# Moving twelve gate mixes from the last attention steps into the value half, with three smaller changes of order

## The chip, the cores and the metric

The kernel runs on one core of one Trainium2 chip. The metric is device time in microseconds (us) of the whole launch, from the runs listed below. Engines are named TensorE (PE, with its weight loads PEld), VectorE (DVE), ScalarE (ACT), GpSimd (POOL) and SyncE (SP), which issues most DMAs in the order of its queue.

## What is computed

The reference is an attention whose scores are capped by a tanh, followed by a channel mix with a gate (batch 8, 12 heads, 448 positions, head size 64, model width 768, inner width 1024):

```
scores = cap * tanh(q k^T / sqrt(64) / cap)
attn   = softmax(scores);  x = attn v, heads side by side   # (8, 448, 768)
x_prev = x shifted by one position (zeros first)
xk = mu_k * x + (1 - mu_k) * x_prev;  xr = mu_r * x + (1 - mu_r) * x_prev
k  = relu(xk @ w_k);  v = k*k @ w_v;  r = sigmoid(xr @ w_r)
out = r * v
```

All is float32. Products that need it are made of three products of high and low parts (high x high, low x high, high x low).

## The kernel before

The order of all instructions is written out by hand; each engine runs its own in that order.

**Attention, steps 0 to 54.** 48 pairs of heads go through a software pipeline. The string `STEP` lists the operations of one step; an operation works on pair i, i-1 or i-2. Scores of pair i come in four groups (`S0` to `S3`), each followed on ScalarE by `tanh` and `exp` and on VectorE by `red` (row sums). In the next step `values` (`V`) makes the value product, `gather` collects the sums over SyncE (four small DMAs), `recip` inverts them on VectorE, and `rec_store` and `rec_load` (SyncE) spread the result over the partitions through device memory. In the step after that `norm` multiplies, `mix_old` (ScalarE) and `mix_new` (VectorE) make xk in the bank of the value product and so free it, `x_high` and `x_low` (GpSimd) split xk, and `gate_old` (GpSimd) and `gate_new` (VectorE) make xr, which `x_store` writes to device memory (`x_d`). Seven steps behind, `kpart` (`K`, four times in a step) makes the products with w_k; `relu` empties finished ones and `k_store` writes them (`k_d`). The weights are handed over as 64-bit numbers and are turned into float32 between these, until about step 40. There are no scores after step 47; steps 48 to 54 finish the pairs and the K products.

**The twelve early pairs.** For pairs 0 to 11 `gate_old` and `gate_new` are left out, and `x_store` writes the plain x to `raw_d`. Their gate mix is made later: from step 36 on `late_load` brings a tile back, `late_old` and `late_new` mix it in steps 37 to 48, and `late_store` writes it to `x_d`.

**Change of stage.** At step 49 (`tail`) the attention's buffers are closed, the halves of w_v are loaded (`w2_loads`, four DMAs of 768 KB), and `w2_prep` makes from them the seven factors of a Strassen product in high and low parts: 22 pieces, six behind each of the steps 50 to 53.

**Value half, then gate half.** 14 units of 256 tokens each. A unit has seven slots, one for each of seven products (`multiply`; 12 matmuls in the value half, 9 in the gate half). `ahead` prepares operands two slots early (high part on ScalarE, low part on VectorE), loads sources and, in the value half, squares them. `evacuate` empties the banks a slot after a product. w_r is loaded at the start of the value half (`w2_loads`, four DMAs of 576 KB) and prepared during it. A slot was emitted in this order: multiply, ahead, evacuate, stores.

Of the kernel before, what the change touches and what calls it, by code (L numbers as in the profile page):

```python
# [10 lines left out]
F32 = mybir.dt.float32  # L11
F32R = mybir.dt.float32r
AF = mybir.ActivationFunctionType
ALU = mybir.AluOpType
# [3 lines left out]
B, H, S, D = 8, 12, 448, 64  # L18
# [25 lines left out]
NB = 2 * S // 32  # L44
P1, P2, P3, P4, P5, P6, P7 = range(7)
LATE = 12
AT = NPAIR + 1 - LATE

STEP = """gather load_v weight_load more weight_low S0 S1 V S2 f f f f f tanh0 exp0 red0
weight_sum tanh1 exp1 red1 norm recip rec_store K qk_high qk_low tanh2 mix_old mix_new x_high x_low gate_old late_old relu k_store
K exp2 red2 weight_rest weight_sum relu k_store S3 K K tanh3 exp3 red3 gate_new late_new relu k_store weight_abs load_qk rec_load x_store late_store late_load weight_store"""


def f(ap):
    return ap.bitcast(F32)  # L60


class Body:
# [54 lines left out]
    def init_x(self, pool):  # L118
        self.X = []
        for j in range(2):  # L120
            x = pool.tile([P, S + 1], F32, name=f"x{j}", bufs=1)
            self.nc.vector.memset(x[:, 0:1], 0.0)
            self.X.append(x)
        self.xo = pool.tile([P, S + 1], F32, name="xo", bufs=1)
        self.nc.vector.memset(self.xo[:, 0:1], 0.0)

    def init_sums(self, pool):

# [185 lines left out]
            self.nc.sync.dma_start(self.raw_d[i], self.X[i % 2][:, 1:])  # L314

    def late_load(self, i):
        if i < LATE:
            self.nc.sync.dma_start(self.xo[:, 1:], self.raw_d[i])

    def late_old(self, i):  # L320
        if i < LATE:
            self.xl = self.up.tile([P, S], F32, name="xl", bufs=1)
            self.nc.gpsimd.tensor_scalar(self.xl, self.xo[:, 0:S], self.om["r"][:, i % NP:i % NP + 1], None, op0=ALU.mult)

    def late_new(self, i):
        if i < LATE:
            self.mix_gate(self.xo, self.xl, i % NP)

    def late_store(self, i):
        if i < LATE:  # L330
            self.nc.sync.dma_start(self.x_place(i), self.xl)

    def key_order(self):

# [116 lines left out]
        next(self.wgen)  # L451


    def w2_pool(self, kind, pool):
        n = (NF if kind == "v" else ND) // 2
        self.W2[kind] = lo, hi = {}, {}
        for x, w in (("l", lo), ("h", hi)):
            for m in (P1, P7, P3, P2, P5, P6, P4):
                w[m] = pool[x].tile([P, n, HN], F32R, name=f"w{kind}{x}{m}")

    def w2_loads(self, kind):
        lo = self.W2[kind][0]
        n, at = lo[P1].shape[1], (ND if kind == "v" else 0)
        for m, c, h in ((P1, 0, 0), (P7, 0, 1), (P3, n, 1), (P2, n, 0)):
            self.nc.sync.dma_start(f(lo[m]), self.w_d[at + c:at + c + n, :, h * HN:(h + 1) * HN].rearrange("c p n -> p c n"))

    def w2_split(self, kind, m, k, x=None):
        lo, hi = (w[m][:, k] for w in self.W2[kind])
        x = f(lo) if x is None else x
        self.nc.scalar.copy(hi, x)  # L470
        self.nc.vector.tensor_sub(lo, x, f(hi))

    def w2_prep(self, kind, scratch, k):

        a, b = scratch
        b11, b12, b22, b21 = (f(self.W2[kind][0][m][:, k]) for m in (P1, P7, P3, P2))
        for m, x, sub in ((P5, a, (a, b12, b11)), (P1, None, ()), (P6, b, (b, b22, a)), (P5, a, ()), (P4, a, (a, b21, b)),
                          (P6, b, ()), (P7, b, (b, b22, b12)), (P7, b, ()), (P2, None, ()), (P4, a, ()), (P3, None, ())):
            if sub:
                self.nc.vector.tensor_sub(*sub)  # L480
            else:
                self.w2_split(kind, m, k, x)
            yield
# [51 lines left out]
    def multiply(self, u, i):  # L535
        m, n = self.products(u)[i], self.half(u)
        hi, lo = self.ops.pop((u, i))
        wl, wh = (w[m] for w in self.W2["v" if u < NU else "r"])
        bank = {P1: 0, P2: 0, P6: 1, P7: 1, P5: 2, P3: 2, P4: 3}[m]
        first = (u, bank) not in self.ps  # L540
        if first:
            self.ps[u, bank] = self.ps_2.tile([P, 512], F32, name="ps2")
        o = self.ps[u, bank][:, 0:HN]
        last = not first or bank == 3
        todo = [(hi, w, c) for c in range(n) for w in (wh, wl)] + [(lo, wh, c) for c in range(n)]
        for k, (a, w, c) in enumerate(todo):
            self.nc.tensor.matmul(o, a[:, c, :], w[:, c, :], start=first and k == 0, stop=last and k == len(todo) - 1,  # L547
                                  skip_group_check=True)
# [65 lines left out]

    def slot(self, g):
        u, s = divmod(g, SLOTS)
        if u < 2 * NU:
            self.multiply(u, s)
            self.ahead(g)
        now, self.later = self.later, []  # L620
        if g and g <= 2 * NU * SLOTS:
            v, r = divmod(g - 1, SLOTS)
            self.evacuate(v, self.products(v)[r])
        for do, args in now:
            do(*args)


    def step(self, i, KS):

        nk = 0  # L630
        if self.maxima and i < NPAIR:
            self.row_maxima(i)
        pair = dict(load_qk=i + 3, qk_high=i + 2, qk_low=i + 2, load_v=i, S=i, tanh=i, exp=i, red=i)
        pair.update(dict.fromkeys("V gather recip rec_store rec_load".split(), i - 1))
        pair.update(dict.fromkeys("norm mix_old mix_new x_high x_low gate_old gate_new x_store".split(), i - 2))
        pair.update(dict.fromkeys("late_old late_new late_store".split(), i - AT), late_load=i + 1 - AT)
        for op in STEP.split():
            j = pair.get(op)
            op, g = (op[:-1], (int(op[-1]),)) if op[-1].isdigit() else (op, ())
            if op in pair:  # L640
                j = pair[op] if j is None else j
                if 0 <= j < NPAIR:
                    getattr(self, dict(S="scores", V="values").get(op, op))(j, *g)
            elif op == "K":
                if i >= LAG:
                    n = ((i - LAG) * 4 + nk) * KS
                    self.kpart(n, n + KS)
                nk += 1
            elif op == "f":
                if i <= NPAIR:  # L650
                    self.fill()
            elif op == "more":
                if i in (6, 7, 8, 9, 10):
                    self.weight_load()
            else:
                getattr(self, op)()

    def run(self):
# [7 lines left out]
        with ExitStack() as outer:  # L666
# [41 lines left out]
            tail = NPAIR + 1  # L708
            self.later = []
            first = -12  # L710
            for i in range(NPAIR + LAG):
                if i == tail:
                    self.weight_store()
                    assert self.w_next == NW and not (self.w_raw or self.w_abs or self.w_sum or self.w_low)
                    wst.close()
                    est.close()
                    ast.close()
                    tiles = dict(right, reuse_waits="tile")
                    self.w2_pool("v", {x: pool("w2v" + x, 1, **tiles) for x in "lh"})
                    self.srcp = pool("srcp", 2, **tiles)  # L720
                    self.sp = pool("sp", 1, **tiles)
                    self.evp = pool("evp", 1, **tiles)
                    self.w2_loads("v")
                    t = self.srcp.tile([P, NF, 2 * P], F32, name="src").rearrange("p (a n) t -> p a (n t)", a=2)
                    scratch = [t[:, j, :2 * HN].rearrange("p (n t) -> p n t", n=2) for j in range(2)]
                    prep = chain(*(self.w2_prep("v", scratch, slice(j, j + 2)) for j in (0, 2)))
                self.step(i, KS)
                if i == tail:
# [1 line left out]
                    sst.close()  # L730
                    self.opp = pool("opp", AHEAD + 1, **tiles)
                    self.ps_2 = pool("ps2", 6, space=PSUM, **right)
                else:
                    for _ in range(6 if i > tail else 0):
                        next(prep, None)
                if i > tail:
                    for g in range(first, min(first + 3, 0)):
# [8 lines left out]
            self.w2_pool("r", dict(l=w2r, h=w2r))  # L746
# [3 lines left out]
            st_pool = pool("st", 1, st)  # L750
            self.w2_loads("r")
            prep = self.w2_prep("r", [st_pool.tile([P, ND // 2, HN], F32, name=f"st{j}") for j in range(2)], slice(0, ND // 2))
            for g in range(2 * NU * SLOTS + 3):
                self.slot(g)
                if g > SLOTS and g % SLOTS == 3:
                    next(prep, None)
                if g == NU * SLOTS - 9:
                    assert next(prep, None) is None
# [58 lines left out]
```

## Time and profile before

| | |
|---|---|
| time, median of 3 runs | 981.52 us (979.04 to 981.6) |
| profiled execution, its own time | 978.96 us |
| its span, first to last instruction | 977.2 us |
| mean granted clock of TensorE | 0.977 |
| busy: TensorE, VectorE, ScalarE, GpSimd | 93%, 78%, 64%, 43% |

A page of the profile gives busy time as a share of the span; the end of a matmul is modelled, so a busy TensorE is not one at its peak. A row of a timeline has the start, the duration, the engine, the line, the operation with its tiles and, in brackets, how long the engine was idle before it and what ended that. A granted clock of 1.00 is 2.4 GHz and 0.50 is 1.2 GHz.

### The profile page before, as it was taken

What the parts mean: (1) busy time and instruction counts of PE and PEld (TensorE: products, weight loads), DVE (VectorE), ACT (ScalarE), POOL (GpSimd) and SP (SyncE); (2) the same over time, 40 slices, a digit from 0 to 9 for tenths busy, and PEclk for the clock granted to TensorE, in tenths of its full rate; (3) what the DMA queues carried; (4) which work ended last, traced back from release to release, by engine and by line L of the source; (5) the groups of instructions that cost most, each with busy time, mean ns of one, the idle gap of its engine ahead of it and who ended that gap; (6) DMA issues with size and microseconds to landing.
All of it is one profiled execution on the core that took longest, in us unless ns stands there. A gap on an engine that the chain in (4) does not pass through costs nothing. (4 is left out here: it accounts for less than half of the span.)

```text
span 977.2 us, 15124 instructions
## 1 busy us (share of the span) xinstructions
PE 907.9 (93%) x4986; PEld 719.7 (74%) x4986; DVE 757.6 (78%) x1262; ACT 624.0 (64%) x915; POOL 416.8 (43%) x362
## 2 busy tenths in 40 slices
PE   6778989999999999989889887999999999999996
PEld 3336656666666766656556676999999999999996
DVE  7999998888888888887776565777777766777775
ACT  7887668877887788777667244455546535554443
POOL 4666656666766776676664310000000013433330
PEclk9889999999999999999999999899999999999999
DMA  5556446665666666665553374433433436666663
GB/s 157 173 183 200 161 146 206 196 201 176 212 207 209 192 202 209 196 204 170 170 159 132 122 248 168 139 118 123 146 113 120 151 104 195 204 207 203 206 201 109
DMA packets 122008, 169.46 MB, mean 173 GB/s; under 512 B 22464, under 2 KB 106048, under 8 KB 121920
## 3 DMA queue, kind: packets, MB, share of 16 engines
q1 hardware_dynamic: 112704, 153.72, 49.7%
q10 hardware_dynamic: 9216, 14.68, 4.1%
q8 instruction: 41, 0.67, 0.3%
q14 instruction: 47, 0.39, 0.1%
HBM read 109.45 MB, written 56.14 MB: 169 GB/s over the span
## 5 line engine op out<-in xcount | busy, mean ns | idle before, releaser
L243 DVE TRANSPOSE_TENSOR_REDUCE r<-p 128x28 f32<-128x896 f32 (+1 forms) x240 | 216.0, 914 | 26.6 <-ACT p L217 22.6
L217 ACT ACTIVATE p<-p,cap_t 128x896 f32<-128x896 f32 x192 | 182.1, 948 | 13.4 <-ACT ko L361 8.6
L207 ACT ACTIVATE p<-s,scl_t 128x896 f32<-128x896 f32 x192 | 173.2, 902 | 21.2 <-PE s L199 13.8
L354 PE MATMUL kps<-xkh,wkh 128*128 128x448 f32 x384 | 147.6, 384 | 13.0 <-ACT ko L361 9.1
L354 PE MATMUL kps<-xkl,wkh 128*128 128x448 f32 x384 | 142.5, 371 | 1.1 <-POOL xkl L87 1.1
L354 PE MATMUL kps<-xkh,wkl 128*128 128x448 f32 x384 | 141.9, 370 | 0.0
L547 PE MATMUL ps<-wvh,hi 128*128 128x384 f32 x392 | 132.8, 339 | 7.0 <-ACT hi L531 5.6
L226 PE MATMUL pv<-p,rv 128*64 128x448 f32 x576 | 128.0, 582 | 5.1 <-DVE xk L283 4.6
L547 PE MATMUL ps<-wvl,hi 128*128 128x384 f32 x392 | 132.3, 337 | 0.0
L511 POOL TENSOR_TENSOR s<-src 128x384 f32<-128x384 f32 x14 | 14.3, 1025 | 275.3 <-DVE lo L532 271.3
L531 ACT CAST hi<-s 128x512 fp32r<-128x512 f32 (+1 forms) x112 | 63.5, 567 | 103.0 <-PE ps L547 87.9
L532 DVE TENSOR_TENSOR lo<-s,hi 128x512 fp32r<-128x512 f32 (+1 forms) x112 | 71.1, 635 | 63.4 <-ACT hi L531 53.5
L199 PE MATMUL s<-qkh 64*128 64x448 f32 (+1 forms) x336 | 84.8, 447 | 29.0 <-ACT p L207 24.2
L87 POOL TENSOR_TENSOR qkl<-rqk,qkh 128x960 fp32r<-128x960 f32 x47 | 107.7, 2291 | 3.9
L547 PE MATMUL ps<-wrh,hi 128*128 128x384 f32 x294 | 99.8, 340 | 5.6 <-DVE u L566 5.3
L428 POOL TENSOR_TENSOR wsq<-wa,wsq 128x384 f32<-128x384 f32 x44 | 44.7, 1016 | 136.0 <-DVE wsq L421 131.9
L199 PEld LDWEIGHTS s<-qkh 64*128 64x128 f32 (+1 forms) x336 | 36.8, 188 | 88.9 <-ACT p L207 41.0
L547 PE MATMUL ps<-wrl,hi 128*128 128x384 f32 x294 | 98.8, 336 | 0.0
L354 PEld LDWEIGHTS kps<-xkh,wkh 128*128 128x128 f32 x384 | 73.0, 190 | 34.8 <-issue 12.9
L531 ACT CAST hi<-src 128x512 fp32r<-128x512 f32 (+1 forms) x84 | 47.7, 568 | 69.5 <-PE ps L547 58.2
L226 PEld LDWEIGHTS pv<-p,rv 128*64 128x64 f32 x576 | 39.6, 144 | 71.0 <-issue 60.8
L278 ACT ACTIVATE pv<-x,om_k 128x448 f32<-128x448 f32 x48 | 30.6, 638 | 93.8 <-DVE x L268 93.8
(88 smaller groups left out, 1856.0 us busy)
## 6 DMA issues: line engine op xcount, KB each, us to landing
rqk<-qk SPq DMA_DIRECT2D x47, 480.0 KB
k_d<-ko ACTq DMA_DIRECT2D x64, 224.0 KB
src<-k_d SPq DMA_DIRECT2D x56, 256.0 KB
rv<-v SPq DMA_DIRECT2D x48, 256.0 KB
r<-rec_d SPq DMA_DIRECT2D x96, 112.0 KB
v_d<-o SPq DMA_DIRECT2D x56, 192.0 KB
src<-x_d SPq DMA_DIRECT2D x42, 256.0 KB
vl<-v_d SPq DMA_DIRECT2D x56, 192.0 KB
```

The source lines that it names most:

```text
L87: {"p": self.nc.gpsimd, "v": self.nc.vector}[e].tensor_sub(*a)
L199: nc.tensor.matmul(s[:, h, 0:S], qk[a][p, k], qk[b][p, 0:S], start=(n == 0), stop=(n == 2))
L207: self.nc.scalar.activation(p32, self.S.pop((i, g))[:, :n, 0:S], AF.Tanh, scale=self.scl_t)
L217: self.nc.scalar.activation(p32, p32, AF.Exp, scale=1.0 if self.maxima else self.cap_t)
L226: nc.tensor.matmul(pv[p, 0:S], v[:, g, h, :], ph[:, h, :], start=(g == 0), stop=False)
L243: self.nc.vector.tensor_reduce(out=out, in_=p32[p, h].rearrange("p h (b k) -> p (h b) k", k=32), axis=mybir.AxisListType.X, op=ALU.add, ap ...
L278: self.nc.scalar.mul(self.xold, self.X[i % 2][:, 0:S], self.om["k"][:, hp:hp + 1])
L354: nc.tensor.matmul(self.kps[fc][:, 0:S], w, m[:, dc, :], start=first, stop=last)
L428: {"p": self.nc.gpsimd, "v": self.nc.vector}[e].tensor_add(sq, f(a), sq)
L531: self.nc.scalar.copy(hi, x)
L532: self.nc.vector.tensor_sub(lo, x, f(hi))
L547: self.nc.tensor.matmul(o, a[:, c, :], w[:, c, :], start=first and k == 0, stop=last and k == len(todo) - 1, skip_group_check=True)
```

## The change

1. The late mixes leave the steps. `late_load` is emitted in slot 0 and the new `late_mix` in slot 2 of the value units 0 to 11. The multiply that GpSimd did is done by ScalarE. Their tiles come from a pool of that stage, and to make room for it the preparation of w_r works on one block of rows at a time, in 33 pieces instead of 11, emitted in three slots of a unit instead of one.
2. `relu` in the second line of `STEP` is emitted behind `tanh2` instead of behind the mixes.
3. The loads of w_v are emitted in step 48, behind `V` (`tail_open`), instead of at the start of step 49; six pieces of the preparation are emitted behind step 49 already.
4. In the gate half, `evacuate` is emitted ahead of `ahead` in slot 2.

```
-STEP = """gather load_v weight_load more weight_low S0 S1 V S2 f f f f f tanh0 exp0 red0
-weight_sum tanh1 exp1 red1 norm recip rec_store K qk_high qk_low tanh2 mix_old mix_new x_high x_low gate_old late_old relu k_store
-K exp2 red2 weight_rest weight_sum relu k_store S3 K K tanh3 exp3 red3 gate_new late_new relu k_store weight_abs load_qk rec_load x_store late_store late_load weight_store"""
+STEP = """gather load_v weight_load more weight_low S0 S1 V tail_open S2 f f f f f tanh0 exp0 red0
+weight_sum tanh1 exp1 red1 norm recip rec_store K qk_high qk_low tanh2 relu mix_old k_store mix_new x_high x_low gate_old
+K exp2 red2 weight_rest weight_sum relu k_store S3 K K tanh3 exp3 red3 gate_new relu k_store weight_abs load_qk rec_load x_store weight_store"""
...
-    def late_old(self, i):
...
-            self.nc.gpsimd.tensor_scalar(self.xl, self.xo[:, 0:S], self.om["r"][:, i % NP:i % NP + 1], None, op0=ALU.mult)
...
+    def late_mix(self, i):
+        x = self.latep.tile([P, S], F32, name="xl")
+        self.nc.scalar.mul(x, self.xo[:, 0:S], self.om["r"][:, i % NP:i % NP + 1])
+        self.mix_gate(self.xo, x, i % NP)
+        self.nc.sync.dma_start(self.x_place(i), x)
...
     def slot(self, g):
         u, s = divmod(g, SLOTS)
+        now, self.later = self.later, []
         if u < 2 * NU:
             self.multiply(u, s)
-            self.ahead(g)
-        now, self.later = self.later, []
+            if u < NU or s != 2:
+                self.ahead(g)
         if g and g <= 2 * NU * SLOTS:
             v, r = divmod(g - 1, SLOTS)
             self.evacuate(v, self.products(v)[r])
+        if NU <= u < 2 * NU and s == 2:
+            self.ahead(g)
+        if u < LATE and s == 0:
+            self.late_load(u)
+        if u < LATE and s == 2:
+            self.late_mix(u)
         for do, args in now:
             do(*args)
...
+    def tail_open(self, i):
+        if i == NPAIR:
+            self.weight_store()
...
+            self.open_tail()
...
+            def tail_open():
+                ast.close()
+                self.w2v = {"l": pool("w2vl", 1, **tiles)}
+                self.w2_pool("v", "l", self.w2v)
+                self.w2_loads("v")
+            self.open_tail = tail_open
...
-                else:
-                    for _ in range(6 if i > tail else 0):
+                if i >= tail:
+                    for _ in range(6):
                         next(prep, None)
...
-            prep = self.w2_prep("r", [st_pool.tile([P, ND // 2, HN], F32, name=f"st{j}") for j in range(2)], slice(0, ND // 2))
+            scratch = [st_pool.tile([P, 1, HN], F32, name=f"st{j}") for j in range(2)]
+            prep = chain(*(self.w2_prep("r", scratch, slice(j, j + 1)) for j in range(ND // 2)))
             for g in range(2 * NU * SLOTS + 3):
                 self.slot(g)
-                if g > SLOTS and g % SLOTS == 3:
+                if g > SLOTS and g % SLOTS in (1, 3, 5):
                     next(prep, None)
```

## Rows read from the trace of the kernel before

**Rows 1.** The page's first part: busy time, share of the span and instructions of each engine.

```profile
PE 907.9 (93%) x4986; PEld 719.7 (74%) x4986; DVE 757.6 (78%) x1262; ACT 624.0 (64%) x915; POOL 416.8 (43%) x362
```

**Rows 2.** Busy time by stretches: from and to, length, busy time of each engine with its instructions, granted clock, DMA share and rate. In order: steps 13 to 34; the K products of the last batch; the start of the value half; the rest of the value half; the gate half.

```profile
157.50:397.70 240.20, 239.37 (x1349) 162.95 (x1347) 204.66 (x352) 194.64 (x252) 160.53 (x132) 1.00 0.62 198
...
566.00:592.50 26.50, 25.90 (x120) 23.13 (x118) 19.25 (x22) 15.37 (x24) 2.10 (x2) 0.94 0.58 208
592.50:618.50 26.00, 18.60 (x85) 17.29 (x85) 13.43 (x22) 10.56 (x20) 0.00 (x0) 0.87 0.61 198
618.50:807.70 189.20, 189.20 (x1093) 189.10 (x1093) 137.51 (x216) 98.33 (x172) 4.32 (x4) 1.00 0.40 126
807.70:969.70 162.00, 156.28 (x884) 152.22 (x882) 120.82 (x222) 80.45 (x166) 56.18 (x52) 1.00 0.61 192
```

**Rows 3.** Timeline of VectorE: `mix_new` (line 283), which comes once in a step. The rows are those of pairs 11, 33, 34 and 45, in steps 13, 35, 36 and 47.

```profile
157.47 0.63 DVE L283 SCALAR_TENSOR_TENSOR xk<-x,mu_k,pv 128x448 f32<-128x448 f32 x1
...
397.73 0.63 DVE L283 SCALAR_TENSOR_TENSOR xk<-x,mu_k,pv 128x448 f32<-128x448 f32 x1
...
408.14 0.63 DVE L283 SCALAR_TENSOR_TENSOR xk<-x,mu_k,pv 128x448 f32<-128x448 f32 x1
...
544.98 0.63 DVE L283 SCALAR_TENSOR_TENSOR xk<-x,mu_k,pv 128x448 f32<-128x448 f32 x1
```

**Rows 4.** Timeline of SyncE's queue at the end of an earlier step (two rows) and of a late step (four rows), and three rows of the waits from 425 to 550 us (engine and line that waited, what it waited for, us in total, times, longest).

```profile
314.43 0.33 SPq L312 DMA_DIRECT2D x_d<-xg  x1
...
315.32 2.44 SPq L248 DMA_DIRECT2D sq<-r  x4
...
500.98 0.33 SPq L312 DMA_DIRECT2D x_d<-xg  x1
502.72 0.33 SPq L331 DMA_DIRECT2D x_d<-xl  x1
503.13 0.38 SPq L318 DMA_DIRECT2D xo<-raw_d  x1
503.57 2.44 SPq L248 DMA_DIRECT2D sq<-r  x4
...
ACT pv L278 <- DVE x L268: 28.7, 10, 4.3
DVE sr L252 <- DMA sq<-r: 19.6, 10, 2.7
...
PE kps L354 <- ACT ko L361: 5.3, 2, 3.0
```

**Rows 5.** Timelines around steps 47 to 49: SyncE's queue (the store of pair 45's gate mix, `gather`, `rec_store` and `rec_load` of pair 47, the loads of w_v), then VectorE (`recip` and `norm` of pair 47, the first piece of the preparation), then TensorE (the first K product that needs pair 47).

```profile
549.98 0.33 SPq L312 DMA_DIRECT2D x_d<-xg  x1
...
551.84 2.45 SPq L248 DMA_DIRECT2D sq<-r  x4
557.02 0.33 SPq L259 DMA_DIRECT2D rec_d<-rs  x1
558.64 1.12 SPq L264 DMA_DIRECT2D r<-rec_d  x2
...
563.38 2.30 SPq L465 DMA_DIRECT2D wvl<-w_d  x4
...
555.80 0.61 DVE L252 TENSOR_REDUCE sr<-sq 32x28 f32<-32x448 f32 x1 [4.30 <-DMA sq<-r]
...
562.84 0.62 DVE L268 TENSOR_TENSOR x<-pv,r 128x448 f32<-128x448 f32 x1
...
570.22 0.96 DVE L480 TENSOR_TENSOR src<-wvl,wvl 128x768 f32<-128x768 f32 x1 [1.40 <-DMA wvl<-w_d]
...
565.55 0.47 PE L354 MATMUL kps<-xkh,wkh 128*128 128x448 f32 x1 [3.77 <-POOL xkh L77]
```

**Rows 6.** Timelines at the start of the value half: ScalarE's queue (the last store of K products), SyncE's queue (loads of w_r, then the last quarter of unit 1's source), ScalarE (the square that reads it), TensorE (the last K product; the first matmul of unit 1).

```profile
598.72 0.33 ACTq L367 DMA_DIRECT2D k_d<-ko  x1
...
600.80 2.09 SPq L465 DMA_DIRECT2D wrl<-w_d  x4
602.93 0.49 SPq L491 DMA_DIRECT2D src<-k_d  x1
...
610.30 0.63 ACT L496 ACTIVATE src<-src 128x512 f32<-128x512 f32 x1 [7.58 <-DMA src<-k_d]
...
592.21 0.36 PE L354 MATMUL kps<-xkl,wkh 128*128 128x448 f32 x1
...
618.51 0.33 PE L547 MATMUL ps<-wvh,hi 128*128 128x384 f32 x1
```

**Rows 7.** The gate half: a low part on VectorE and TensorE's first matmul of slot 3 behind it, from the timelines, and one row of the waits from 807 to 977 us.

```profile
868.05 1.30 DVE L532 TENSOR_TENSOR lo<-src,hi 128x384 fp32r<-128x384 f32 x1 [0.50 <-ACT hi L531]
...
869.97 0.41 PE L547 MATMUL ps<-wrh,hi 128*128 128x384 f32 x1 [0.46 <-DVE u L566]
...
PE ps L547 <- DVE u L566: 5.3, 11, 0.7
```

**Rows 8.** Groups of instructions over the whole span: line, engine, operation, tiles, shapes and count, then busy us and mean ns of one, then the idle time before them and what ended it.

```profile
L566 DVE TENSOR_TENSOR u<-ps,p 128x384 f32<-128x384 f32 x56 | 30.7, 549 | 0.0
L278 ACT ACTIVATE pv<-x,om_k 128x448 f32<-128x448 f32 x48 | 30.6, 638 | 93.8 <-DVE x L268 93.8
...
L295 DVE SCALAR_TENSOR_TENSOR xl<-xo,mu_r,xl 128x448 f32<-128x448 f32 x12 | 12.5, 1045 | 3.6 <-POOL xl L323 3.6
```

More of the change, by code (lines that the diff above doesn't have):

```diff
@@ L46 @@
 LATE = 12
-AT = NPAIR + 1 - LATE
-STEP = """gather load_v weight_load more weight_low S0 S1 V S2 f f f f f tanh0 exp0 red0
-weight_sum tanh1 exp1 red1 norm recip rec_store K qk_high qk_low tanh2 mix_old mix_new x_high x_low gate_old late_old relu k_store
-K exp2 red2 weight_rest weight_sum relu k_store S3 K K tanh3 exp3 red3 gate_new late_new relu k_store weight_abs load_qk rec_load x_store late_store late_load weight_store"""
+STEP = """gather load_v weight_load more weight_low S0 S1 V tail_open S2 f f f f f tanh0 exp0 red0
+weight_sum tanh1 exp1 red1 norm recip rec_store K qk_high qk_low tanh2 relu mix_old k_store mix_new x_high x_low gate_old
+K exp2 red2 weight_rest weight_sum relu k_store S3 K K tanh3 exp3 red3 gate_new relu k_store weight_abs load_qk rec_load x_store weight_store"""
 def f(ap):
@@ L123, in init_x @@
             self.X.append(x)
-        self.xo = pool.tile([P, S + 1], F32, name="xo", bufs=1)
-        self.nc.vector.memset(self.xo[:, 0:1], 0.0)
     def init_sums(self, pool):
@@ L316, in late_load @@
     def late_load(self, i):
-        if i < LATE:
-            self.nc.sync.dma_start(self.xo[:, 1:], self.raw_d[i])
-    def late_old(self, i):
-        if i < LATE:
-            self.xl = self.up.tile([P, S], F32, name="xl", bufs=1)
-            self.nc.gpsimd.tensor_scalar(self.xl, self.xo[:, 0:S], self.om["r"][:, i % NP:i % NP + 1], None, op0=ALU.mult)
[L325 to L331, printed above, removed]
+        self.nc.sync.dma_start(self.xo[:, 1:], self.raw_d[i])
+    def late_mix(self, i):
[3 more added lines that the diff above has]
+        self.nc.sync.dma_start(self.x_place(i), x)
     def key_order(self):
@@ L451, in fill, with w2_pool @@
         next(self.wgen)
-    def w2_pool(self, kind, pool):
+    def w2_pool(self, kind, x, pool):
         n = (NF if kind == "v" else ND) // 2
[L456 to L459, printed above, removed]
+        self.W2[kind, x] = {m: pool[x].tile([P, n, HN], F32R, name=f"w{kind}{x}{m}") for m in (P1, P7, P3, P2, P5, P6, P4)}
     def w2_loads(self, kind):
-        lo = self.W2[kind][0]
+        lo = self.W2[kind, "l"]
         n, at = lo[P1].shape[1], (ND if kind == "v" else 0)
@@ L467, in w2_split @@
     def w2_split(self, kind, m, k, x=None):
-        lo, hi = (w[m][:, k] for w in self.W2[kind])
+        lo, hi = (self.W2[kind, a][m][:, k] for a in "lh")
         x = f(lo) if x is None else x
@@ L475, in w2_prep @@
         a, b = scratch
-        b11, b12, b22, b21 = (f(self.W2[kind][0][m][:, k]) for m in (P1, P7, P3, P2))
+        b11, b12, b22, b21 = (f(self.W2[kind, "l"][m][:, k]) for m in (P1, P7, P3, P2))
         for m, x, sub in ((P5, a, (a, b12, b11)), (P1, None, ()), (P6, b, (b, b22, a)), (P5, a, ()), (P4, a, (a, b21, b)),
@@ L537, in multiply @@
         hi, lo = self.ops.pop((u, i))
-        wl, wh = (w[m] for w in self.W2["v" if u < NU else "r"])
+        wl, wh = (self.W2["v" if u < NU else "r", a][m] for a in "lh")
         bank = {P1: 0, P2: 0, P6: 1, P7: 1, P5: 2, P3: 2, P4: 3}[m]
@@ L623, in slot @@
             self.evacuate(v, self.products(v)[r])
+        if NU <= u < 2 * NU and s == 2:
[4 more added lines that the diff above has]
+            self.late_mix(u)
         for do, args in now:
             do(*args)
+    def tail_open(self, i):
+        if i == NPAIR:
+            self.weight_store()
+            assert self.w_next == NW and not (self.w_raw or self.w_abs or self.w_sum or self.w_low)
+            self.open_tail()
     def step(self, i, KS):
@@ L635, in step @@
         pair.update(dict.fromkeys("norm mix_old mix_new x_high x_low gate_old gate_new x_store".split(), i - 2))
-        pair.update(dict.fromkeys("late_old late_new late_store".split(), i - AT), late_load=i + 1 - AT)
         for op in STEP.split():
@@ L648, in step @@
                 nk += 1
+            elif op == "tail_open":
+                self.tail_open(i)
             elif op == "f":
@@ L710, in run @@
             first = -12
+            tiles = dict(right, reuse_waits="tile")
+            def tail_open():
[4 more added lines that the diff above has]
+            self.open_tail = tail_open
             for i in range(NPAIR + LAG):
                 if i == tail:
-                    self.weight_store()
-                    assert self.w_next == NW and not (self.w_raw or self.w_abs or self.w_sum or self.w_low)
                     wst.close()
                     est.close()
-                    ast.close()
-                    tiles = dict(right, reuse_waits="tile")
-                    self.w2_pool("v", {x: pool("w2v" + x, 1, **tiles) for x in "lh"})
+                    self.w2v["h"] = pool("w2vh", 1, **tiles)
+                    self.w2_pool("v", "h", self.w2v)
                     self.srcp = pool("srcp", 2, **tiles)
@@ L722, in run @@
                     self.evp = pool("evp", 1, **tiles)
-                    self.w2_loads("v")
                     t = self.srcp.tile([P, NF, 2 * P], F32, name="src").rearrange("p (a n) t -> p a (n t)", a=2)
@@ L745, in run @@
             w2r = pool("w2r", 1)
-            self.w2_pool("r", dict(l=w2r, h=w2r))
+            for a in "lh":
+                self.w2_pool("r", a, {a: w2r})
             self.outp = pool("outp", 4)
@@ L750, in run @@
             st_pool = pool("st", 1, st)
+            self.latep = pool("latep", 1, st)
+            self.xo = self.latep.tile([P, S + 1], F32, name="xo")
+            nc.vector.memset(self.xo[:, 0:1], 0.0)
             self.w2_loads("r")
-            prep = self.w2_prep("r", [st_pool.tile([P, ND // 2, HN], F32, name=f"st{j}") for j in range(2)], slice(0, ND // 2))
+            scratch = [st_pool.tile([P, 1, HN], F32, name=f"st{j}") for j in range(2)]
+            prep = chain(*(self.w2_prep("r", scratch, slice(j, j + 1)) for j in range(ND // 2)))
             for g in range(2 * NU * SLOTS + 3):
                 self.slot(g)
-                if g > SLOTS and g % SLOTS == 3:
+                if g > SLOTS and g % SLOTS in (1, 3, 5):
                     next(prep, None)
```

## The prediction

> **What bounds the kernel now.** I read the page first, then the busy time by stages, then the waits and the timelines of the stages that have gaps. TensorE is busy for 93% of the span [rows 1], so an edit pays only where TensorE stands idle or is slow. The table by stages says where that is [rows 2]: steps 13 to 34 keep it busy for 239.37 of 240.20 us and the value half, once it runs, for all of 189.20 us. The gaps are in the last attention steps, at the change from attention to the value half (18.60 busy of 26.00 us, at a granted clock of 0.87) and, thinly, in the gate half (156.28 of 162.00).
>
> The late steps show best in the start of `mix_new` on VectorE, which comes once in a step [rows 3]: 157.47 to 397.73 us are 22 steps of 10.92 us, in which TensorE is full, so 10.92 us is TensorE's own pace. From 408.14 to 544.98 us are 11 steps of 12.44 us with the same matmuls. SyncE's queue shows why [rows 4]. In an undisturbed step the store of the gate mix goes out at 314.43 us and the first `gather` 0.89 us later. In a late step the store goes out at 500.98, then the queue stands at `late_store` until 502.72, issues `late_load` at 503.13 and reaches `gather` at 503.57 us, 2.59 us after. What `gather` brings ends VectorE's wait for `recip` in 10 steps of that stretch, 19.6 us in all; `mix_new` stands behind `recip`, and `values` needs the bank that `mix_new` frees. So a loop through SyncE's queue, not TensorE, sets the late steps.
>
> **Late mixes.** Removed from these steps: on SyncE a store and a load each, on GpSimd and VectorE one mix each. The queue gets back 2.59 - 0.89 = 1.7 us, and 12.44 - 1.7 = 10.74 us lies under TensorE's pace. The steps should fall to 10.92 us: 11 x (12.44 - 10.92) = **16.7 us** less by the last full step. Bounds: if another link holds them near 11.6, 9 us; if the 1.7 us comes back whole, 18.7 us.
>
> In the value half they come back as 12 ScalarE multiplies of 0.638 us (the nearest row is the same shape at L278) and 12 VectorE mixes of at most 1.045 us [rows 8]. The w_r preparation does its columns in 33 VectorE instructions of 384 columns, 0.549 us by the nearest row; counted as if all were new, VectorE goes from 137.51 us to 137.5 + 12.5 + 18.1 = 168 of 189.2 us, and ScalarE from 98.3 to 106 and some more smaller copies [rows 2, 8]. Operands are made two slots ahead, so I price this at **0**, 0 to 3 us. Its cover is the full TensorE; without that it would cost 12 x (0.638 + 1.045) = 20 us.
>
> **Relu behind the third tanh.** On ScalarE it now stands ahead of `mix_old`, which waits 28.7 us in 10 steps for the normalisation [rows 4], more than 0.5 us in each: a relu fits there and delays nothing. It frees a product's bank earlier; TensorE's two waits on that (5.3 us) lie in the late steps and are in the 16.7. **0**, with 3 us of gain as the far bound; if the normalisation stopped being late, each relu would push `mix_old` back by its own length in half of the steps, but there TensorE is full.
>
> **Value weights in step 48.** This edit moves four loads of 768 KB on SyncE's queue ahead of `rec_store`, `rec_load` and `x_store` of that step. The first load is free at once; the second waits for `values` of pair 47, which ends at about the time at which `gather` is through. I count from the store at 549.98 us as if nothing before it had moved [rows 5]. `gather` follows at 550.4 instead of 551.84, its four issues take 2.45 us, and the four weight loads occupy the queue from 552.8 to 555.1. `recip` ran 3.96 us after the first `gather` issue, so 554.3, and `rec_store` is issued at 555.5. Its 3.5 KB lie behind 3 MB. What that costs shows at 600.80 us [rows 6]: four loads of 576 KB, then a 256 KB load at 602.93, and its reader starts at 610.30, 9.5 us after the first issue. That is 9.5 us for 2.62 MB, hence 11.4 us for 3.15 MB: `rec_store` lands at about 564.2. SyncE waits for that before `rec_load` (1.1 us for two issues, and 1.5 us to land, as the last `gather` took from 554.29 to 555.80). The normalisation of pair 47 starts at 566.8 instead of 562.84, and the K matmuls that wait for it, 2.71 us behind [rows 5], at 569.5 instead of 565.55: **+4.0 us**. Bounds: if small transfers pass the weights, `rec_load` goes out at 557.1, the normalisation at 560.0, and it is -2.8 us; the far end is +5.5 us, with a longer low clock behind the longer gap.
>
> The Trainium skill ("DMA: Bandwidth & Descriptors", section "Queues, rings and completion order") speaks against this edit too: descriptors of one issuing engine's row are taken in ring order on each DMA engine, and a completion lands only after the earlier writes of that engine. By that rule this term is +4.0 us and not -2.8. The trace agrees for a load behind loads (the 9.5 us above); a store behind loads it does not show.
>
> **Preparation and the start of the value half.** Preparation stands behind `gate_new` of pair 47 in VectorE's order and today waits only 1.40 us for the weights at 570.22 [rows 5]; whatever the weights do, it moves with the normalisation. But six of its 22 pieces are now in step 49 instead of behind the K products of step 50, the weights lie ready, and it ends a step earlier, ahead of the last K matmul. Today that is not so: from the last K matmul at 592.21 to unit 1 at 618.51 are 26.3 us [rows 6], for seven slots of 2.08 us (12 matmuls of 189.20 / 1093 = 0.173 us [rows 2]). ScalarE is late with the last relu, its store goes out at 598.72 and lands before SyncE's loads of w_r at 600.80; behind these lies the last quarter of unit 1's source, and ScalarE's queue stands at its square until 610.30. In the new order the last relu follows the K end by some 0.7 us: store, 2.1 us to land, w_r loads at +2.9, the source at +12.4 (9.5 more), its square 0.5, the first late multiply 1.3 with what its own load takes longer, the next operand 0.5: TensorE's sixth slot starts 14.6 us after the K end, the last two slots take 4.2, and the low clock after the shorter gap some 1.7 (today 0.13 of 26 us, 3.4, part of it while idle [rows 2]). That is 20.5 instead of 26.3: **-5.8 us**, bounds -3 and -8.
>
> **A sum ahead of operands.** In slot 2 of a gate unit VectorE adds P6 to P1 behind an operand's low part, which takes 1.30 us at 868.05; TensorE then waits for that sum, 11 times, 5.3 us in all [rows 7]. Emitted first it is done a slot earlier. The gate half has 882 matmuls of 0.173 us, 153 us, in a stretch of 162.00 [rows 2], so more hangs on those stops than the idle time says: each also costs the overlap of 0.33 - 0.173 = 0.16 us [rows 6] and a slow restart of 0.41 - 0.33 = 0.08, 7.9 us together. The operand that is now later is needed two slots on. **-7 us**, bounds -4 and -8.
>
> **Sum.** -16.7 + 4.0 - 5.8 - 7.0 = -25.5 us on a profiled execution of 978.96 us: 953.5. The median of before, 981.52, stands 2.6 us above that execution; I take half of this and say **955 us**.
>
> **Rivals.** *The weights hold nothing up* (chance 0.2): small packets pass, the term is -2.8 instead of +4.0, and the time is 948. For it: today `rec_load` follows `rec_store` by 1.6 us; against it: 610.30.
> *The late steps keep part of their length* (0.15): another link of the loop, GpSimd's gate mix or ScalarE, is just behind SyncE, steps stay at 11.6, and the gate gives 4: 979 - 9 + 4 - 6 - 4 = 964, 965 as a median. Against it: steps 13 to 34 carry more work on VectorE at 10.92.
> *Slower* (0.04): ScalarE stands at the late multiply in slot 2 until the raw tile is in. The load is issued in slot 0, some 5 us before; 2.9 us more (two slots of 2.08 less high and low part) are covered; each unit must lose 25.5 / 12 = 2.1 us, so a landing 10 us after issue, in every unit, undoes all. DMA is at 0.40 there [rows 2]; above 982 us from then on.
> *The change does not do what it says* (0.05): late mixes and weights leave the steps, but the pace of the late steps is that of a chain that has nothing to do with SyncE; then the gate half and the tail leave 979 - 7 + 4 - 6 to 979 + 4 - 4, so 970 to 979.
>
> **How the numbers follow.** My forecast, 950 to 960, has 0.56. The range of 944 to 967 takes in the first two rivals nearly whole. 0.3% (3 us) is what a measurement can tell here: faster 0.93, same 0.03, slower 0.04.
>
> **What would show it.** `mix_new` every 10.9 us up to step 47; `gather` right behind `x_store`; a gap of TensorE of about 8 us before the K products of the last batch, longer than today's 3.8, with the normalisation of pair 47 some 4 us later against the store of pair 45; no stop for an operand in the first two value slots; w_r loads 3 us behind the last K matmul; no wait for the sum in the gate half; TensorE without gaps in units 1 to 11. Late steps above 11.3 us, or the normalisation early, would break the first or third term.

## The result, and the profile after

The changed kernel takes 955.4 us (median of 4 runs, 950.45 to 957.79) against 980.28 us (4 runs of the kernel before beside it): a ratio of 0.974, 95% interval 0.9697 to 0.9784. Its profiled execution, 957.79 us, is the slowest of its four. The forecast was 955, in the range of 944 to 967.

The page's first part, as [rows 1]:

```profile
span 955.9 us, 15133 instructions
...
PE 898.6 (94%) x4986; PEld 720.9 (75%) x4986; DVE 748.6 (78%) x1284; ACT 632.8 (66%) x941; POOL 400.1 (42%) x350
```

Busy time by stretches, columns as in [rows 2]; the stretches are cut at events: `mix_new` of pairs 11, 34 and 45; the store of pair 45's gate mix; the first K product that needs pair 47; the end of the K products; the first matmul of unit 1; the first of the gate half; its end.

```profile
158.80:407.00 248.20, 248.16 (x1412) 171.16 (x1411) 214.40 (x368) 203.83 (x262) 167.13 (x138) 1.00 0.62 200
407.00:525.90 118.90, 118.39 (x671) 81.78 (x670) 87.89 (x138) 94.44 (x119) 68.64 (x55) 1.00 0.48 156
530.50:551.40 20.90, 9.81 (x49) 8.47 (x47) 4.30 (x8) 3.12 (x5) 3.68 (x4) 0.87 0.61 210
551.40:583.80 32.40, 29.09 (x121) 25.23 (x122) 23.10 (x27) 17.52 (x27) 2.53 (x2) 0.88 0.32 106
583.80:605.06 21.26, 17.43 (x86) 17.11 (x84) 10.22 (x18) 8.53 (x16) 0.00 (x0) 0.84 0.66 222
605.06:794.40 189.34, 189.34 (x1094) 189.24 (x1093) 145.24 (x249) 105.93 (x197) 4.35 (x4) 1.00 0.47 154
794.40:948.00 153.60, 153.28 (x883) 152.67 (x882) 115.44 (x221) 80.27 (x166) 55.80 (x52) 1.00 0.64 202
```

The late steps are full now and the gate half has lost its gaps, but the change of stage has new ones: half of the time around 540 us is idle, and the K products of the last batch take 32.2 us at a granted clock of 0.88, where they took 26.7 at 0.94 before.

The timelines name the events. VectorE's `mix_new` of pair 34, then SyncE's queue in a late step, to be read against [rows 3, 4]:

```profile
407.02 0.63 DVE L280 SCALAR_TENSOR_TENSOR xk<-x,mu_k,pv 128x448 f32<-128x448 f32 x1
...
488.49 0.33 SPq L309 DMA_DIRECT2D x_d<-xg  x1
488.87 2.44 SPq L245 DMA_DIRECT2D sq<-r  x4
```

Steps 47 to 49, against [rows 5]: SyncE's queue from the store of pair 45's gate mix on, VectorE (`mix_new` of pair 45, `recip` and `norm` of pair 47), ScalarE, then TensorE.

```profile
530.51 0.34 SPq L309 DMA_DIRECT2D x_d<-xg  x1
530.94 2.44 SPq L245 DMA_DIRECT2D sq<-r  x4
533.49 2.56 SPq L451 DMA_DIRECT2D wvl<-w_d  x4
536.15 0.94 SPq L256 DMA_DIRECT2D rec_d<-rs  x1
545.14 1.12 SPq L261 DMA_DIRECT2D r<-rec_d  x2
...
525.87 0.63 DVE L280 SCALAR_TENSOR_TENSOR xk<-x,mu_k,pv 128x448 f32<-128x448 f32 x1
...
534.71 0.61 DVE L249 TENSOR_REDUCE sr<-sq 32x28 f32<-32x448 f32 x1 [2.60 <-DMA sq<-r]
...
548.66 0.62 DVE L265 TENSOR_TENSOR x<-pv,r 128x448 f32<-128x448 f32 x1 [8.20 <-DMA r<-rec_d]
...
555.56 0.83 ACT L456 CAST wvh<-src 128x768 fp32r<-128x768 f32 x1 [4.85 <-DVE src L466]
...
558.23 0.54 ACT L350 ACTIVATE ko<-kps 128x448 f32<-128x448 f32 x1
...
551.38 0.74 PE L343 MATMUL kps<-xkh,wkh 128*128 128x448 f32 x1 [10.68 <-POOL xkh L76]
...
556.09 0.37 PE L343 MATMUL kps<-xkl,wkh 128*128 128x448 f32 x1
558.82 0.47 PE L343 MATMUL kps<-xkh,wkh 128*128 128x448 f32 x1 [2.35 <-ACT ko L350]
...
559.96 0.57 PE L343 MATMUL kps<-xkh,wkl 128*128 128x448 f32 x1
```

`gather` follows the store by 0.38 us in the late step and by 0.43 behind pair 45's. But between `rec_store` and `rec_load` lie 9.0 us instead of 1.6; VectorE waits 8.20 us for `rec_load`, and TensorE 10.68. A second, smaller stop follows: ScalarE stands at a copy of the preparation (4.85 us, for VectorE), the relu behind it comes at 558.23, and TensorE has waited 2.35 us for its bank; after each of the two stops a matmul holds TensorE for 0.57 us instead of 0.36. The granted clock behind the second stop, columns as above:

```profile
559.58:562.60 3.02, 3.02 (x10) 2.66 (x9) 2.08 (x3) 1.58 (x3) 0.00 (x0) 0.50 0.49 186
```

Stretch by stretch, before and after, in us:

| from, to | before | after | difference |
|---|---|---|---|
| start to `mix_new` of pair 11 | 157.5 | 158.8 | +1.3 |
| to pair 34 | 250.7 | 248.2 | -2.5 |
| to pair 45 | 136.8 | 118.8 | -18.0 |
| to the first K product that needs pair 47 | 20.6 | 25.5 | +4.9 |
| to the last K product | 26.7 | 32.2 | +5.5 |
| to unit 1 of the value half | 26.3 | 21.5 | -4.8 |
| to the gate half | 189.3 | 189.3 | 0.0 |
| to the end of the span | 169.3 | 161.5 | -7.8 |

But for rounding the rows add up to the 21.3 us by which the spans differ; the medians differ by 24.9. One execution fixes such a stretch to some 3 us only: in the nine kernels of this document that have the relu early, the start up to pair 11 takes 155.9 to 158.8 us and pair 34 to pair 45 takes 116.5 to 119.1, with the same order of instructions there.

### The profile page after: what moved, and what is told of

Same layout as the page of the kernel before. It is cut to its first block, busy times and chain, and to the rows that moved or that the text cites. A ratio compares the mean times of both kernels' runs of the same rounds, so it can differ in the third digit from the quotient of the medians.

```text
span 955.9 us, 15133 instructions
## 1 busy us (share of the span) xinstructions
PE 898.6 (94%) x4986; PEld 720.9 (75%) x4986; DVE 748.6 (78%) x1284; ACT 632.8 (66%) x941; POOL 400.1 (42%) x350
## 4 chain that ended last, share of the span: by engine, by line
PE 48%; DVE 16%; POOL 13%; DMA 6%; issue 6%; SPq 5%; ACT 4%; ACTq 0%; DVEq 0%; POOLq 0%
PE ps L533 36%; PE kps L343 5%; SPq L245 4%; POOL xg L298 4%; DMA sq<-r 4%; PE pv L223 3%; POOL xkl L86 3%; DVE r L240 3%; PE s L196 3%; POOL qkl L86 2%; DVE xg L292 2%; POOL xkh L76 2%; ACT p L214 2%; DVE xk L280 2%; DVE sr L249 2%
## 5 line engine op out<-in xcount | busy, mean ns | idle before, releaser
L343 PE MATMUL kps<-xkh,wkh 128*128 128x448 f32 x384 | 146.2, 381 | 13.9 <-POOL xkh L76 10.7
L533 PE MATMUL ps<-wvh,lo 128*128 128x384 f32 x392 | 84.4, 336 | 0.0
```

The costliest lines, as they stand in the source:

```text
L343: nc.tensor.matmul(self.kps[fc][:, 0:S], w, m[:, dc, :], start=first, stop=last)
```

## The experiments

Theory: SyncE's queue set the late steps, and each other part does what its own stretch shows, with the weights in step 48 as a loss. Rivals: the gain of the late steps comes from another part; the gap at 540 us comes from elsewhere; the early preparation pays.

**Only the late mixes moved.** The changed kernel with its parts 2, 3 and 4 undone.

> Only the late mixes are moved (with the w_r preparation cut finer for their room); the relu, the loads of w_v, the preparation and the sum stand as before. Theory: SyncE's queue set the late steps, so the normal pace of 10.8 to 10.9 us returns from pair 34 to pair 45, the store of pair 45's gate mix comes 17 to 19 us earlier, and nothing is given back in the value half: 958 to 964 us. Rival: the steps were short of something else (the relu's place or the pace of TensorE), and the pace stays above 11.6 us: 968 to 980 us.

960.25 us (ratio to before 0.9782, 0.9752 to 0.9811). From `mix_new` of pair 34 to that of pair 45 it takes 118.9 us, as the changed kernel does (10.8 us a step). From the last K matmul to the gate half, with the late mixes in it, are 216.5 us, against 215.6 before. So the first part alone is some 20 us, and the rival falls. Which of the pieces that left set the late steps, SyncE's store and load or the mixes on GpSimd and VectorE that the store waited for, no run separates; the rows of [rows 4] speak for the queue.

**The weights back in step 49.**

```
-STEP = """gather ... S0 S1 V tail_open S2 ... red0
+STEP = """gather ... S0 S1 V S2 ... red0
...
                 if i == tail:
+                    self.tail_open(NPAIR)
                     wst.close()
...
-                if i >= tail:
+                if i > tail:
                     for _ in range(6):
                         next(prep, None)
```

> The changed kernel with its third part undone: loads of w_v at the start of step 49 again and preparation from step 50 on. Theory: the weights ahead of rec_store cost more than the early preparation gives. The normalisation of pair 47 starts about 11 us behind the store of pair 45's gate mix instead of 18.1, TensorE's gap before the last batch is under 4 us instead of 10.7, the K products of the last batch take some 26.7 us instead of 32.2, and the start of the value half is as slow as in the kernel before (26 us from the last K matmul to unit 1 instead of 21.5): 943 to 950 us. Rival: the gap comes from elsewhere and the early weights do pay: 956 to 962 us.

945.36 us (0.9645, 0.9611 to 0.9678), 10 us faster than the changed kernel. In the profiled executions the three stretches from pair 45 to unit 1, which the edit touches, give 6.9 us of that. SyncE's queue, then TensorE's stops before the last batch:

```profile
525.83 0.34 SPq L309 DMA_DIRECT2D x_d<-xg  x1
526.27 2.46 SPq L245 DMA_DIRECT2D sq<-r  x4
531.27 0.33 SPq L256 DMA_DIRECT2D rec_d<-rs  x1
532.56 1.12 SPq L261 DMA_DIRECT2D r<-rec_d  x2
535.84 0.33 SPq L309 DMA_DIRECT2D x_d<-xg  x1
536.27 2.56 SPq L451 DMA_DIRECT2D wvl<-w_d  x4
...
539.10 0.47 PE L343 MATMUL kps<-xkh,wkh 128*128 128x448 f32 x1 [2.12 <-POOL xkh L76]
540.34 0.74 PE L343 MATMUL kps<-xkl,wkh 128*128 128x448 f32 x1 [0.57 <-POOL xkl L86]
```

`rec_load` follows `rec_store` by 1.3 us, the normalisation starts 10.55 us behind the store of pair 45's gate mix (12.86 before, 18.15 after), and the gap is 2.1 us. The K products take 28.3 us, the start of the value half 26.0.

**Only the preparation put back.** The loads stay in step 48.

```
-                if i >= tail:
+                if i > tail:
```

> The changed kernel with the six early pieces of the preparation put back behind step 50; the loads stay in step 48. Theory: the gap of 10.7 us stays, since the loads make it, but the stop of 2.35 us at 558.8 us (a bank that waits for a relu, which stands behind the preparation on ScalarE) goes, the K products take 28 to 30 us instead of 32.2, and the value half starts some 2 us worse: within 3 us of the changed kernel. Rival: that stop is made by the slow clock alone; then K products take 32 us again and the kernel is 2 to 4 us slower than the changed one.

954.19 us (0.9729, 0.9701 to 0.9756), no different from the changed kernel. TensorE's only stop before and in the K products, from the timeline:

```profile
547.10 0.74 PE L343 MATMUL kps<-xkh,wkh 128*128 128x448 f32 x1 [10.53 <-POOL xkh L76]
```

and the busy time of their stretch:

```profile
547.10:575.00 27.90, 27.73 (x120) 24.35 (x120) 19.22 (x22) 15.43 (x24) 2.53 (x2) 0.89 0.28 96
```

The gap of 10.5 us stays, the stop for the relu goes: 27.6 us for the K products instead of 32.2. The start of the value half is back at 25.4 us instead of 21.5. What the early pieces give there, they had taken from the K products.

**The sum behind the operands again.**

```
-            if u < NU or s != 2:
-                self.ahead(g)
+            self.ahead(g)
...
-        if NU <= u < 2 * NU and s == 2:
-            self.ahead(g)
```

> The changed kernel with its fourth part undone: in the gate half the sum is emitted behind the operand again. Theory: TensorE waits for that sum in slot 3 of most units again, the gate half takes 161 to 162 us instead of 153.3, the kernel 962 to 965 us. Rival: the gate half is shorter for another reason (the transfers or preparation ahead of it): under 158 us, 955 to 959 us in all.

962.82 us (0.9816, 0.9786 to 0.9846). The waits of its gate half have the line of [rows 7] back, and from its first to its last matmul it takes 161.9 us instead of 153.3.

```profile
PE ps L533 <- DVE u L552: 5.5, 12, 0.5
```

**Half of the weights early.** Two loads in step 48, two at the start of step 49.

```
...
-                self.w2_loads("v")
+                self.w2_loads("v", slice(0, 2))
...
                 if i == tail:
+                    self.w2_loads("v", slice(2, 4))
```

> The changed kernel with only two of the four loads of w_v (1.57 MB) in step 48; the other two are at the start of step 49. Theory: rec_store waits for what lies ahead of it on SyncE's row, in proportion to its bytes: from the first of these loads to rec_load 5.5 to 6.5 us instead of 11.65, so the normalisation of pair 47 comes 5 to 6 us earlier against the store of pair 45's gate mix, TensorE's gap is about 5 us instead of 10.7, and the kernel gains 3 to 6 us on the changed one. Rival: the wait is a fixed one (any large load ahead holds the small one up): rec_load still some 11 us after the first load, no gain.

949.76 us (0.9681, 0.9647 to 0.9714). SyncE's queue:

```profile
527.11 0.34 SPq L309 DMA_DIRECT2D x_d<-xg  x1
527.55 2.44 SPq L245 DMA_DIRECT2D sq<-r  x4
530.09 1.07 SPq L451 DMA_DIRECT2D wvl<-w_d  x2
532.53 0.33 SPq L256 DMA_DIRECT2D rec_d<-rs  x1
537.80 1.12 SPq L261 DMA_DIRECT2D r<-rec_d  x2
```

From the first load to `rec_load` 7.7 us, where 3.15 MB cost 11.65: more than the 5.5 to 6.5 expected, but it goes with the bytes, 3.9 us for 1.57 MB or 2.5 us for a MB. The normalisation starts 14.2 us behind the store of pair 45's gate mix (18.15), and TensorE's gap is 5.8 us. The rival of a fixed wait falls.

**The weights on ScalarE's queue.** Same place in the program, issued by ScalarE.

```
-            self.nc.sync.dma_start(f(lo[m]), self.w_d[at + c:at + c + n, :, h * HN:(h + 1) * HN].rearrange("c p n -> p c n"))
+            (self.nc.scalar if kind == "v" else self.nc.sync).dma_start(f(lo[m]), self.w_d[at + c:at + c + n, :, h * HN:(h + 1) * HN].rearrange("c p n -> p c n"))
```

> The changed kernel with the four loads of w_v issued by ScalarE at the same place of the program instead of by SyncE. Theory: rec_store waits because it lies behind 3 MB on the same row of rings; on another row it shares the engines packet by packet, rec_load follows rec_store by 1.5 to 4 us instead of 9.0, TensorE's gap falls to 3 to 6 us and the kernel gains 4 to 8 us on the changed one. Rival (the Trainium skill, DMA: Bandwidth & Descriptors, Queues, rings and completion order: a completion lands only after every earlier write of that DMA engine, across its queues): rec_load still comes 7 us or more after rec_store and nothing is gained.

952.98 us (0.9716, 0.968 to 0.9751), a gain of 2.4 us, less than the theory's 4 to 8 and not clear of the spread of the changed kernel. SyncE's queue, ScalarE's queue, VectorE's waits:

```profile
528.62 0.34 SPq L309 DMA_DIRECT2D x_d<-xg  x1
529.05 2.49 SPq L245 DMA_DIRECT2D sq<-r  x4
537.63 0.33 SPq L256 DMA_DIRECT2D rec_d<-rs  x1
541.68 1.11 SPq L261 DMA_DIRECT2D r<-rec_d  x2
...
528.44 7.85 ACTq L451 DMA_DIRECT2D wvl<-w_d  x4
...
536.41 0.61 DVE L249 TENSOR_REDUCE sr<-sq 32x28 f32<-32x448 f32 x1 [6.29 <-DMA sq<-r]
...
545.19 0.62 DVE L265 TENSOR_TENSOR x<-pv,r 128x448 f32<-128x448 f32 x1 [3.03 <-DMA r<-rec_d]
```

`rec_load` follows `rec_store` by 4.05 us instead of 9.0, and the rival's 7 us are not seen. But no part of that is shown to come from the other queue: when `rec_store` goes out at 537.63, only 0.81 MB of the weights are still to move, against 2.94 MB at that place in the changed kernel and 1.49 MB in half_loads (worked out from the DMA packets of the traces, as the next times are). The small store did not pass what was left. Its first packet starts at 540.61, behind the last packet of the weights at 540.43; in the changed kernel its packets start at 544.22 to 544.45 and the last one of the weights ends at 544.67.

`gather`, issued just behind the first two loads, fares alike. Its packets start at 533.40 to 535.47, and by then 1.55 of the 1.57 MB of those loads have moved; in the changed kernel its first packet starts 1.2 us behind its first issue, here 4.3. `recip` starts 7.4 us after that issue instead of 3.8, so the normalisation starts 16.6 us behind the store, against 18.15 and 10.55. So the theory that small transfers get past the weights on another queue is not borne out here; what `rec_store` no longer waits, `gather` mostly waits. ScalarE also stands at its second load until `values` is done, and TensorE waits 3.61 us for a relu behind it.

**Unit 1's source ahead of the weights of the gate.**

```
+            self.src_load(1, 3)
+            self.late_load(0)
             self.w2_loads("r")
...
-        if u is not None and s < 4:
+        if u is not None and s < 4 and (u, s) != (1, 3):
...
-        if u < LATE and s == 0:
+        if 0 < u < LATE and s == 0:
```

> The changed kernel with two small loads emitted ahead of the loads of w_r: the last quarter of unit 1's source and the first raw tile. Theory: ScalarE's wait of 7.8 us at the square of that quarter, and TensorE's of 3.8 us behind it with the slow clock that follows, come from the place behind 2.36 MB in SyncE's queue; without it the stretch from the last K matmul to unit 1 is 15 to 17 us instead of 21.5, and the kernel gains 4 to 7 us. Rival: the stop at the sixth slot is one of operands (VectorE or ScalarE late for another reason): under 2 us.

947.62 us (0.9657, 0.9626 to 0.9688), 7.8 us faster than the changed kernel. The last K matmul and the first matmul of unit 1:

```profile
581.45 0.36 PE L343 MATMUL kps<-xkl,wkh 128*128 128x448 f32 x1
...
596.23 0.33 PE L533 MATMUL ps<-wvh,hi 128*128 128x384 f32 x1
```

Between them lie 14.8 us instead of 21.5, and TensorE has no stop left there. Seven slots of 2.08 us are 14.6.

**The relu behind the mixes again.**

```
-weight_sum ... tanh2 relu mix_old k_store mix_new x_high x_low gate_old
+weight_sum ... tanh2 mix_old mix_new x_high x_low gate_old relu k_store
```

> The changed kernel with its second part undone: the relu stands behind the mixes again. Theory: the relu's place is worth nothing in steps that TensorE fills; pair 11 to pair 34 takes 248 us as in the changed kernel (250.7 in the kernel before), and the whole is within 2 us of the changed kernel. Rival: the earlier relu freed banks earlier; then 2 to 4 us come back as a loss, half of it between pairs 11 and 34.

959.13 us (0.9779, 0.9751 to 0.9806), 3.7 us above the changed kernel; the intervals of the two overlap, so the stretch has to decide. From pair 11 to pair 34 it takes 250.3 us. Over all kernels the relu's place sorts that stretch: 250.0 to 250.7 us in the three with the old place (before, late_only, undo_relu), 247.3 to 248.7 in the nine others. The rival is right. The waits from 157 to 408 us in undo_relu:

```profile
PEld kps L343 <- ACT ko L350: 2.6, 3, 1.2
...
PE kps L343 <- ACT ko L350: 1.5, 3, 0.8
```

and in the changed kernel, where these two are gone and the wait goes the other way:

```profile
ACT ko L350 <- PE kps L343: 6.7, 15, 1.0
```

In this stretch TensorE never waits for the relu when it is early; the relu waits for TensorE. At the 46 passages from scores to a K product the next matmul starts on average 0.072 us before the modelled end of the last one in undo_relu and 0.116 in the changed kernel (worked out from the timelines). That is 2.0 us, nearly all of it at three passages, where the profile shows 1.45 us as idle; at the others the overlap is the same.

`mix_new` moves a little against TensorE's own order, so the same matmuls measure it better, from the first K product of step 13 to that of step 36: 250.6, 250.5 and 250.9 us with the old place, 247.2 to 248.8 with the new one. From the kernel before to the changed one that is 3.1 us: 0.7 at the passages from scores to K products, 0.8 between scores, and 1.5 between K products, each of which starts some 3 ns sooner, with no idle time in either kernel. Why these are closer is open.

**Both repairs together.** undo_loads and source_first in one kernel.

> The changed kernel with its third part undone (loads of w_v at the start of step 49, preparation from step 50) and, as in source_first, unit 1's last source quarter and the first raw tile ahead of the loads of w_r. Theory: the two gains lie in different stretches and add up, 10 us for the loads and 7 us for the source, less what the late preparation still costs in the first slots (stops of 1.0, 0.4, 1.5 and 1.4 us): 19 to 20 us from the last K matmul to unit 1, 937 to 940 us in all. Rival: the late preparation makes ScalarE and VectorE late enough that the source's place no longer counts: 943 to 946 us.

940.73 us (0.9591, 0.9564 to 0.9619): 14.7 us faster than the changed kernel, 40 faster than the one before. From the last K matmul to unit 1 20.4 us, with stops of 1.06, 0.40, 1.68 and 1.38 us from the late preparation; the theory's 19 to 20 and 937 to 940 us were a little low, and the rival's 943 to 946 begins where the runs end (943.58 is the longest). Alone the two repairs gave 10.0 and 7.8 us, so they do not add up in full.

**Half of the weights right behind `rec_load`.**

```
-K exp2 ... load_qk rec_load x_store weight_store"""
+K exp2 ... load_qk rec_load tail_open x_store weight_store"""
...
```

> As best, but two of the four loads of w_v go out in step 48 right behind rec_load, ahead of that step's x_store; the other two at the start of step 49. Theory: nothing that the normalisation needs lies behind them now, its start stays 10.5 us behind the store of pair 45's gate mix, the first piece of the preparation moves 1 to 2.5 us forward, and the first value slots lose less: 0 to 2 us better than best. Rival: the store of pair 46's gate mix now lies behind 1.57 MB and holds up GpSimd's next gate mix, which shares its tile, and with it the preparation: 1 to 3 us worse than best.

940.38 us (0.9604, 0.9577 to 0.9632): the same as best. Both sides were partly right. The normalisation stays at 10.8 us behind the store, but GpSimd's gate mix of pair 47 waits for the store of pair 46's, which lies behind 1.57 MB:

```profile
543.62 1.41 POOL L298 TENSOR_SCALAR xg<-x,om_r 128x448 f32<-128x448 f32 x1 [3.28 <-DMA x_d<-xg]
```

and the preparation starts at 545.67, 9.2 us behind the normalisation instead of 6.8 in best.

## Why the prediction was right, and where its terms were not

That the total came out so close is luck: errors of both signs met. The terms sum to -25.5 us, the stretches to -21.3, and the changed kernel's median lies 2.4 us below the execution that was profiled.

**Late mixes** (forecast -16.7). Right in mechanism as far as the runs go: `gather` goes out right behind the store, and the pace returns to that of TensorE; late_only shows that the first part does this alone. The size is -18.0 up to pair 45, since the pace there is 10.8 us, not 10.92 (10.6 to 10.8 in the other kernels).

**Relu** (0, with 3 as the far bound). Wrong: 2.5 us between pairs 11 and 34, or 3.1 over the same matmuls, and shown by undo_relu. The step that failed is "there TensorE is full": the stretch counted as busy for 239.37 of 240.20 us was not TensorE's floor. In undo_relu the waits for the relu make 2.0 us of the loss; in the kernel before half of it is in matmuls that count as busy and only follow each other more slowly, and what slows them no run shows.

**Late mixes in the value half** (0): right. Units 1 to 13 take 189.3 us before and after, with VectorE's busy time up from 137.5 to 145.2 us and ScalarE's from 98.3 to 105.9.

**Weights in step 48** (+4.0). Right in mechanism and nearly in size: `rec_load` is issued 11.65 us after the first load, forecast 11.4. Against the store of pair 45 the term is +5.3 (18.15 - 12.86), near my far end; the difference is mostly that the normalisation starts 2.4 us after the last issue of `rec_load`, where I took the 1.5 of `gather`. TensorE's gap is 10.7 us, not about 8. And undo_loads has the normalisation at 10.55, not at 12.86 (late_only at 10.5): without these loads the first part brings it forward, so the loads themselves cost 7.6 us there. The Trainium skill's rule that is cited in the prediction ("DMA: Bandwidth & Descriptors", section "Queues, rings and completion order") agrees with the store behind loads on one row, which completes some 9 us after its issue. With the loads on another row loads_act_queue does not speak against it: there too the store's packets start behind the last of the weights.

**Preparation and start of the value half** (-5.8): -4.8, by the steps I gave: the last relu right behind the K end, w_r loads 3.05 us behind the last K matmul, and the same stop behind them; the sixth slot starts 14.6 us after the last K matmul, as forecast, and what follows takes 6.9 us instead of 5.9, at a granted clock of 0.59. But the term left out what the six early pieces do on ScalarE. They stand ahead of step 50's relu in its order and wait for VectorE; the relu is late, a bank is not free, and TensorE stops for 2.35 us and runs at a granted clock of 0.50 again soon after. All six kernels with the pieces that early have such a stop in these K products, of 2.1 to 2.9 us; the six others have none there. That is +5.5 us in the K products, of which prep_step50 gives 4.6 back while the start of the value half loses 4. Early preparation is worth nothing here. I named the ScalarE multiply as what could stand in a queue's head, and did not ask it of the pieces that moved.

**A sum ahead of operands** (-7.0): -7.8 to the end of the span; undo_sum takes 8.6 us of it back.

So the third part as a whole is a loss, of 10 us by the medians of undo_loads and of 6.9 by the stretches that it touches, where my two terms for it gave a gain of 1.8 (1.4 us of that is time which the first part gives back to `gather`).

## What to carry to other kernels

Before a large load is moved up in a queue, list every small transfer that comes to lie behind it and ask who waits for that; here 3 MB ahead of 3.5 KB held up the normalisation by 7.6 us, and the same loads a few instructions further on did not. Work that is emitted earlier on an in-order engine stands ahead of something: look for the short instruction behind it that frees a buffer. A stretch that a profile calls 99.7% busy can still be 1% too long.

## What the runs showed of the hardware

A small store issued while large loads were under way waited for the bytes that were left: with 2.94 MB to move 9.0 us passed until `rec_load` followed, with 1.49 MB 5.3 us, with none 1.3 to 1.6 us; that is some 2.5 us for a MB between the first two. With the loads on another engine's queue and 0.81 MB left it was 4.05 us, and there too the store's packets started only behind the last packet of the weights; a shorter wait from the other queue itself is not shown. Small transfers that had been ahead of the loads then paid (`gather` to `recip` 7.4 instead of 3.8 us).

A stop of 2.35 us, which ended 7.4 us after one of 10.68 us, was followed by the lower clock again: a matmul held TensorE for 0.37 us just ahead of the stop and for 0.57 from 559.6 us on, at a granted clock of 0.50 (1.2 GHz) up to 562.6 us.
